# A third block size for the expert remainders of a routed expert layer: 192 rows with the weights held still in both layers

## The chip, the core and the metric

The kernel runs on one core of a Trainium2 chip. The metric is device time in microseconds (us) of one execution, taken as the median of several. The core has a matrix engine (TensorE, PE in the profile, with its weight loads listed apart as PEld), a vector engine (VectorE, DVE), a scalar engine (ScalarE, ACT), a general engine (GpSimd, POOL) and a synchronising engine (SyncE, SP) that issues most transfers. Results of PE land in eight banks called ps.

## The reference: windowed attention, then one expert per token

Attention over 8 batches and 8 heads comes first: 512 local queries, each with a window of 32 positions to both sides and 32 global keys, and 32 global queries that see all 544 keys. Its output is a matrix of 4352 rows (8 batches of 544 tokens) and 512 columns. Then every row goes through one of eight experts:

```python
for b in range(B):
    prev_e = -1
    for s in range(S):
        fresh_e = int(np.argmax(logits[b, s]))
        if s == 0 or local_gate[b, s] < 0.5:
            e = fresh_e
        else:
            e = prev_e if prev_e >= 0 else fresh_e
        prev_e = e
        ...
        h = np.maximum(x[b, s] @ w1[e], 0.0)
        out[b, s] = p[e] * (h @ w2[e])
```

Layer 1 (`w1`) takes 512 columns to 1024, layer 2 (`w2`) takes 1024 back to 512. How many rows an expert gets depends on the data. The reference's own inputs give the eight experts 710, 117, 1115, 689, 344, 287, 433 and 657 rows. Cut into blocks of 256 this makes 13 full blocks, and a remainder for each expert of 198, 117, 91, 177, 88, 31, 177 and 145 rows.

## The kernel before: attention, routing, then 21 blocks of rows

**Stages.** The first part (`Attn`) computes the attention and writes its rows, with each row's gate probabilities and number, to a table in memory (`xs`). `Route` then finds for every row its expert and its place, and makes lists of row numbers, one list for each block of at most 256 rows of one expert. `Moe` works through the blocks in a fixed order of slots: three full blocks that begin before the routing is finished, then the eight remainders with full blocks between them, then the other full blocks, as many as the routed counts call for. The remainder blocks stand at places 3, 5, 7, 9, 11, 13, 15 and 17 of the order, one for expert 0 to 7, each followed by a full block.

**One block.** `gather` (L1113) fetches the block's rows by indirect transfers into two tiles `xr`, 128 rows each. `xpose` (L1124 to L1131) turns each by four transposes on PE into columns, and stores them as a rounded part `xh` (ACT, L1126) and the rest `xl` (DVE, L1127). Both are in fp32r, a 32-bit format that PE takes at another pace than plain f32; the profile prints f32 for both. The weights come as eight pieces of 128x1024 from memory and are split in the same way, `hi` by ACT (L1089) and `lo` by DVE or POOL (L1098). A product of two split numbers is three matmuls: hi with hi, lo with hi, hi with lo.

**Layer 1, `mm1`** (L1159). For each of eight groups `fc` of 128 hidden columns, 12 matmuls hold a 128x128 piece of the weights and stream 256 columns, the block's rows. ACT takes the sum with a relu into `hh` (L1161), DVE keeps the rest in `hl` (L1162).

**Layer 2, `mm2`** (L1170). Here `hh` and `hl` are held, 128 rows of the block at a time, and 512 columns of the weights are streamed: 24 matmuls for the first 128 rows, 24 for the other 128. `store` (L1179, L1180) scales the result on ACT and scatters it to the output by an indirect transfer on POOL.

**What sets the order.** All is written out by hand. `whole` runs a block of up to 256 rows: layer 1, the first 24 matmuls of layer 2 with the next block's two `xpose` calls after groups 1 and 3 and its next-but-one `gather` (`ahead`) after group 3, the first `store`, the other 24 matmuls, the second `store`. `hook` runs after each group and makes the next weight piece ready, by the table `SP`. `half` runs a remainder of at most 128 rows in another way: it holds `xh` and `xl` in layer 1 and streams 256 columns of weights (L1233), turns the hidden values back on PE (L1222), and runs 24 matmuls of layer 2.

**The choice at run time.** `block` reads the remainder's row count into a register on every engine. With more than 128 rows, `whole` runs, and else `half`. Both are compiled, one behind the other, for each of the eight remainders.

**Banks.** The results of layer 1 rotate over three banks (`ph`), those of layer 2 over three others (`py`), and the transposes use two (`xtp`).

## Time and profile before

| | us |
|---|---|
| median of three runs | 728.29 |
| the three runs | 728.14, 728.29, 732.7 |
| the execution that was profiled: its own time | 726.73 |
| its span, first to last instruction | 725.0 |
| what lies around the span | 1.73 |

In the profile, PE is busy for 694.1 us of the span, DVE for 494.5, ACT for 410.8 and POOL for 249.5. The granted TensorE clock is 0.99 of full speed over the span. A row of the groups of instructions gives the line in the code, the engine, the operation, the tiles, the shapes, how many there are, the busy time and the mean duration of one. The duration of a matmul or a weight load on PE is longer than the distance to the next one, since they are pipelined: how fast PE goes is read from the starts, or from a run of many.

### The profile page before, as it was taken

How to read it: one execution, taken by the hardware profiler on the slowest of the kernel's cores; microseconds unless marked ns; L12 is line 12 of the kernel's file. 1: busy time of each engine (PE TensorE's matmuls, PEld its weight loads, DVE VectorE, ACT ScalarE, POOL GpSimd, SP SyncE). 2: the span in 40 equal slices, each digit the busy share in tenths (PEclk: the TensorE clock that was granted, in tenths of full speed). 3: DMA queues.
4: the chain of work that ended last, by engine and by line, in shares of the span. 5: the costliest groups of instructions: out<-in, count | busy, mean ns of one | idle time of the engine just before them, and what ended most of it. 6: DMA issues, size and time to landing. Idle time of an engine off the chain costs nothing.

```text
span 725.0 us, 19621 instructions
## 1 busy us (share of the span) xinstructions
PE 694.1 (96%) x7797; PEld 591.5 (82%) x7797; DVE 494.5 (68%) x1203; ACT 410.8 (57%) x724; POOL 249.5 (34%) x337
## 2 busy tenths in 40 slices
PE   9999999999899988899999999999999999999991
PEld 7777777777677767789989898898989988998891
DVE  7868778778888578885557675565858456645570
ACT  4555565554555636455467675566766455645560
POOL 6634434433243555523132332314232322312210
PEclk9999999999999999999999999999999999999996
DMA  8966886866594676675678787767878677567772
GB/s 314 377 248 230 318 288 249 324 251 239 191 350 157 212 240 211 227 252 177 224 246 301 266 295 246 214 216 260 288 270 283 227 239 239 189 212 238 237 207 109
DMA packets 50575, 178.74 MB, mean 247 GB/s; under 512 B 8733, under 2 KB 10013, under 8 KB 46368
## 3 DMA queue, kind: packets, MB, share of 16 engines
q1 hardware_dynamic: 43456, 155.76, 62.2%
q0 software_dynamic: 6720, 21.36, 8.4%
q8 instruction: 71, 1.16, 0.6%
q14 instruction: 40, 0.33, 0.2%
q10 hardware_dynamic: 288, 0.13, 0.1%
HBM read 158.84 MB, written 19.42 MB: 246 GB/s over the span
## 4 chain that ended last, share of the span: by engine, by line
PE 57%; DVE 5%; issue 1%; DMA 1%; POOL 1%; ACT 0%; POOLq 0%; ACTq 0%; SPq 0%
PE ps L1170 26%; PE ps L1159 25%; PE ps L1233 3%; PE ps L1124 2%; DVE wp L1098 2%; DMA raw<-in_w_dram 1%; DVE key L739 0%; PE ps L1222 0%; DVE hl L1162 0%; DVE cid L1011 0%; PE ps L987 0%; POOL out_dram L1180 0%; DVE cid L998 0%; DVE bs L919 0%; DVE nbc L916 0%
## 5 line engine op out<-in xcount | busy, mean ns | idle before, releaser
L1089 ACT CAST wp<-raw 128x1024 fp32r<-128x1024 f32 x176 | 182.9, 1049 | 33.8 <-DMA raw<-in_w_dram 32.6
L1170 PE MATMUL ps<-wp,hh 128*128 128x512 f32 x608 | 195.1, 402 | 0.0
L1098 DVE TENSOR_TENSOR wp<-raw,wp 128x1024 fp32r<-128x1024 f32 x154 | 188.2, 1230 | 8.4 <-ACT wp L1089 7.9
L1159 PE MATMUL ps<-xh,wp 128*128 128x256 f32 x1088 | 154.8, 284 | 6.5 <-DVE hl L1162 5.8
L1159 PEld LDWEIGHTS ps<-xh,wp 128*128 128x128 f32 x1088 | 141.1, 190 | 10.0 <-DVE hl L1162 7.1
L1162 DVE SCALAR_TENSOR_TENSOR hl<-ps,hh 128x256 fp32r<-128x256 f32 x136 | 56.9, 421 | 118.1 <-ACT hh L1161 118.1
L1113 POOL DMA_INDIRECT xr<-xs,idx x46 | 59.9, 1303 | 204.6 <-PE ps L1124 126.5
L1170 PEld LDWEIGHTS ps<-wp,hh 128*128 128x128 f32 x608 | 109.3, 188 | 21.6
L1170 PE MATMUL ps<-wp,hl 128*128 128x512 f32 x304 | 120.3, 396 | 0.0
L1161 ACT ACTIVATE hh<-ps 128x256 fp32r<-128x256 f32 x136 | 51.0, 383 | 75.6 <-PE ps L1159 71.3
L1159 PE MATMUL ps<-xl,wp 128*128 128x256 f32 x544 | 87.4, 283 | 0.0
L190 POOL TENSOR_SCALAR_AFFINE_SELECT qbd<-raw 64x512 f32<-64x512 f32 x62 | 44.5, 718 | 120.3 <-PE ps L242 98.4
L1159 PEld LDWEIGHTS ps<-xl,wp 128*128 128x128 f32 x544 | 74.7, 190 | 0.0
L1098 POOL TENSOR_TENSOR wp<-raw,wp 128x1024 fp32r<-128x1024 f32 x21 | 54.8, 2612 | 51.4 <-ACT wp L1089 19.5
L242 PE MATMUL ps<-kx,qbd 128*64 128x128 f32 x1024 | 71.5, 281 | 0.9 <-issue 0.9
L1180 POOL DMA_INDIRECT out_dram<-y,tk x38 | 40.7, 1072 | 81.7 <-ACT y L1179 66.4
L1170 PEld LDWEIGHTS ps<-wp,hl 128*128 128x128 f32 x304 | 57.1, 188 | 13.6
L242 PEld LDWEIGHTS ps<-kx,qbd 128*64 128x64 f32 x1024 | 55.3, 138 | 11.9 <-issue 7.8
L247 DVE TENSOR_REDUCE mx<-ps 128x4 f32<-128x512 f32 x64 | 43.9, 685 | 27.9 <-PE ps L242 27.8
L253 ACT ACTIVATE pe<-pe 128x512 f32<-128x512 f32 x64 | 40.7, 636 | 29.8 <-DVE pe L249 29.8
L1179 ACT ACTIVATE y<-ps,pp 128x512 f32<-128x512 f32 x38 | 26.0, 685 | 53.3 <-issue 46.9
L249 DVE TENSOR_TENSOR pe<-ps,mx 128x512 f32<-128x512 f32 x64 | 44.0, 688 | 1.6
(214 smaller groups left out, 841.4 us busy)
## 6 DMA issues: line engine op xcount, KB each, us to landing
raw<-in_w_dram SPq DMA_DIRECT2D x179, 512.0 KB, 4.4
v<-in_vw_dram SPq DMA_DIRECT2D x32, 1040.0 KB, 9.2
raw<-in_qk_dram SPq DMA_DIRECT2D x32, 528.0 KB, 7.1
xs<-xa SPq DMA_DIRECT2D x8, 1056.0 KB, 4.7
qgb<-in_qg_dram SPq DMA_DIRECT2D x8, 128.0 KB, 4.2
xr<-xs,idx POOLq DMA_INDIRECT x46, 6.3
out_dram<-y,tk POOLq DMA_INDIRECT x38, 5.6
xs<-xg SPq DMA_DIRECT2D x32, 16.0 KB, 4.1
```

What stands on the lines that cost most here:

```text
L190: self.nc.gpsimd.affine_select(out=out, in_=in_, pattern=pat, compare_op=ALU.is_ge, fill=0.0, base=0, channel_multiplier=0)
L242: nc.tensor.matmul(sp[64 * t2:64 * t2 + 64, t], qbd[:, w], kf[:, f:f + P], start=False, stop=True, skip_group_check=True)
L247: nc.vector.tensor_reduce(out=mx, in_=st["sp"], axis=AX.X, op=ALU.max)
L249: nc.vector.tensor_tensor(out=st["pe"][:, 4 * hb:4 * hb + 4], in0=st["sp"], in1=mx.broadcast_to([P, 4, P]), op=ALU.subtract)
L253: self.nc.scalar.activation(out=pe, in_=pe, func=AF.Exp, scale=SCALE)
L1089: nc.scalar.copy(out=hi, in_=raw)
L1098: (nc.gpsimd if pool else nc.vector).tensor_tensor(out=lo, in0=raw, in1=hi.bitcast(F32), op=ALU.subtract)
L1113: self.nc.gpsimd.indirect_dma_start(out=self.xr[j], out_offset=None, in_=src, in_offset=bass.IndirectOffsetOnAxis(ap=self.rt.idx[:, 2 * i ...
L1159: nc.tensor.matmul(ph, a[:, dc, fs], b_[:, dc], start=(n == 0), stop=(n == 11))
L1161: nc.scalar.activation(out=self.hh[:, fc], in_=ph, func=AF.Relu)
L1162: nc.vector.scalar_tensor_tensor(out=self.hl[:, fc], in0=ph, scalar=0.0, in1=self.hh[:, fc].bitcast(F32), op0=ALU.max, op1=ALU.subtract)
L1170: nc.tensor.matmul(py, a[:, fc, js], b_[:, fs], start=(fc == 0 and k == 0), stop=(fc == 7 and k == 2))
```

## The change: at most 192 rows in a block of its own

A constant `PART = 192` is added. Where a remainder has more than 128 rows, `block` now asks a second time: over 192 rows `whole` runs as before, and with 129 to 192 rows the new function `part` runs.

`mm1` gets a width `n`. In `part` it streams 192 columns in place of 256, and its ACT and DVE results are 192 columns wide. In layer 2 `part` holds the weights, 128x128 at a time, and streams 192 columns of `hh` and `hl`, so that the output comes out turned (columns of the output on the partitions, rows of the block along the free side). It goes in two passes `d` over two groups of 128 output columns each, and each pass fills one bank of `py`. ACT and DVE copy the two halves of a bank to the tile `yT`, which is the `xT` tile of the attention used again. Then `back` turns them by transposes with `idf` into the layout that `store` wants: those of pass 0 stand after group 4 of pass 1, those of pass 1 at the end. Two banks of the `ph` rotation take the turned result, and both `store` calls stand at the end of the block. The next block's first `xpose` stands after group 3 of pass 0, its second one behind pass 1, and `ahead` after it.

```diff
+PART = 192
...
-    def mm1(self, i, fc):
+    def mm1(self, i, fc, n=256):
...
-        ph = self.ph()[:, 0:256]
-        n = 0
+        ph = self.ph()[:, 0:n]
+        hh, hl = self.hh[:, fc, 0:n], self.hl[:, fc, 0:n]
+        g = 0
         for a, b_ in ((hi, self.xh), (lo, self.xh), (hi, self.xl)):
             for dc in range(4):
-                nc.tensor.matmul(ph, a[:, dc, fs], b_[:, dc], start=(n == 0), stop=(n == 11))
+                nc.tensor.matmul(ph, a[:, dc, fs], b_[:, dc, 0:n], start=(g == 0), stop=(g == 11))
...
+    def part(self, i, n):
+        nc = self.nc
+        yT = self.yT
+        for fc in range(8):
+            self.mm1(i, fc, n)
+            self.hook(i, fc)
+        out = []
+
+        def back(c):
+            for j in range(2):
+                nc.tensor.transpose(out[j][:, P * c:P * c + P], yT[:, c, P * j:P * j + P], self.cst.idf)
+        for d in range(2):
+            py = self.py().rearrange("p (c t) -> p c t", c=2)
+            for fc in range(8):
+                hi, lo = self.wp[8 * i + 4 + fc // 2]
+                for c in range(2):
+                    f0 = 512 * (fc % 2) + P * (2 * d + c)
+                    for k, (a, b_) in enumerate(((hi, self.hh), (lo, self.hh), (hi, self.hl))):
+                        nc.tensor.matmul(py[:, c, 0:n], a[:, f0:f0 + P], b_[:, fc, 0:n], start=(fc == 0 and k == 0 and c == 0), stop=(fc == 7 and k == 2),
+                                         skip_group_check=True)
+                if d == 0:
+                    self.hook(i, 8 + fc)
+                    if fc == 3:
+                        self.xpose(i + 1, 0)
+                elif fc == 4:
+                    out += [self.ph() for _ in range(2)]
+                    back(0)
+                    back(1)
+            nc.scalar.copy(out=yT[:, 2 * d, 0:n], in_=py[:, 0, 0:n])
+            nc.vector.tensor_copy(yT[:, 2 * d + 1, 0:n], py[:, 1, 0:n])
+        self.xpose(i + 1, 1)
+        self.ahead(i)
+        back(2)
+        back(3)
+        for j in range(2):
+            self.store(out[j], j)
...
                 self.rem = len(self.wp) + 1
-                self.whole(i)
+                with self.tc.If(self.cv[1 + SLOT[i] - NX] > PART) as full:
+                    self.whole(i)
+                end = self.state()
+                self.reset(st)
+                with full.Else():
+                    self.part(i, PART)
...
+    moe.yT = at.xT
```

**How the order of instructions moves, on PE.** In the names, ps with a number is a bank, wp a split weight piece, hh and hl the two parts of the hidden values, xr the fetched rows of the next block, idf the identity, and xT the tile that holds the turned output. A name stands before a comma where it is streamed, behind it where it is held. In the block of expert 3 before, layer 2 begins with these rows:

```order
L1159 MATMUL ps_66<-xl,wp_4208 128x256 x4
L1170 MATMUL ps_63<-wp_4209,hh 128x512 x2
L1170 MATMUL ps_63<-wp_4209,hl 128x512
L1170 MATMUL ps_63<-wp_4209,hh 128x512 x2
L1170 MATMUL ps_63<-wp_4209,hl 128x512
L1124 MATMUL ps_68<-idf,xr_86 128x128 x4
```

In the new function, the same place of the same block, for one weight piece:

```order
L1161 MATMUL ps_66<-xl,wp_4208 128x192 x4
L1277 MATMUL ps_63<-hh,wp_4209 128x192 x2
L1277 MATMUL ps_63<-hl,wp_4209 128x192
L1277 MATMUL ps_63<-hh,wp_4209 128x192 x2
L1277 MATMUL ps_63<-hl,wp_4209 128x192
L1277 MATMUL ps_63<-hh,wp_4209 128x192 x2
L1277 MATMUL ps_63<-hl,wp_4209 128x192
L1277 MATMUL ps_63<-hh,wp_4209 128x192 x2
L1277 MATMUL ps_63<-hl,wp_4209 128x192
```

Held and streamed operands have changed places, and where a weight piece had six matmuls of 512 columns in a pass, it has twelve of 192.

The second place is ACT at the end of the same block. Before, it ends so:

```order
L1126 CAST xh<-ps_67 128x4x128
L1089 CAST wp_101<-raw_78 128x1024
L1089 CAST wp_4207<-raw_79 128x1024
L1089 CAST wp_4208<-raw_80 128x1024
L1179 ACTIVATE y_4318<-ps_63,pp_92 128x512
L1179 ACTIVATE y_4319<-ps_64,pp_92 128x512
L1295 UNCONDITIONAL_BRANCH
```

and in the new function so:

```order
L1090 CAST wp_101<-raw_78 128x1024
L1090 CAST wp_4207<-raw_79 128x1024
L1090 CAST wp_4208<-raw_80 128x1024
L1287 COPY xT<-ps_63 128x192
L1287 COPY xT<-ps_64 128x192
L1127 CAST xh<-ps_67 128x4x128
L1181 ACTIVATE y_4318<-ps_69,pp_92 128x512
L1181 ACTIVATE y_4319<-ps_65,pp_92 128x512
L1336 UNCONDITIONAL_BRANCH
```

The cast that makes the second half of the next block's `xh` has moved from the middle to behind the weight casts and two new copies, and the first store from the middle to the end.

More of the change, by code (lines that the diff above doesn't have):

```diff
@@ L1154, in mm1 @@
         fs = slice(P * (fc % 2), P * (fc % 2) + P)
-        ph = self.ph()[:, 0:256]
-        n = 0
+        ph = self.ph()[:, 0:n]
+        hh, hl = self.hh[:, fc, 0:n], self.hl[:, fc, 0:n]
+        g = 0
         for a, b_ in ((hi, self.xh), (lo, self.xh), (hi, self.xl)):
             for dc in range(4):
-                nc.tensor.matmul(ph, a[:, dc, fs], b_[:, dc], start=(n == 0), stop=(n == 11))
-                n += 1
-        nc.scalar.activation(out=self.hh[:, fc], in_=ph, func=AF.Relu)
-        nc.vector.scalar_tensor_tensor(out=self.hl[:, fc], in0=ph, scalar=0.0, in1=self.hh[:, fc].bitcast(F32), op0=ALU.max, op1=ALU.subtract)
+                nc.tensor.matmul(ph, a[:, dc, fs], b_[:, dc, 0:n], start=(g == 0), stop=(g == 11))
+                g += 1
+        nc.scalar.activation(out=hh, in_=ph, func=AF.Relu)
+        nc.vector.scalar_tensor_tensor(out=hl, in0=ph, scalar=0.0, in1=hh.bitcast(F32), op0=ALU.max, op1=ALU.subtract)
     def mm2(self, i, py, fc, j):
@@ L1296, in block @@
                 self.rem = len(self.wp) + 1
-                self.whole(i)
+                with self.tc.If(self.cv[1 + SLOT[i] - NX] > PART) as full:
[4 more added lines that the diff above has]
+                    self.part(i, PART)
+                assert len(self.wp) == len(end[1]) and self.nld == end[2]
                 self.rem = -1
```

## The prediction

> **What bounds the kernel now.** I read the shares of the engines first, then the chain that ended last.
>
> ```profile
> PE 694.1 (96%) x7797; PEld 591.5 (82%) x7797; DVE 494.5 (68%) x1203; ACT 410.8 (57%) x724; POOL 249.5 (34%) x337
> ...
> PE ps L1170 26%; PE ps L1159 25%; PE ps L1233 3%; PE ps L1124 2%; DVE wp L1098 2%; DMA raw<-in_w_dram 1%; DVE key L739 0%; PE ps L1222 0%; DVE hl L1162 0%; DVE cid L1011 0%; PE ps L987 0%; POOL out_dram L1180 0%; DVE cid L998 0%; DVE bs L919 0%; DVE nbc L916 0%
> ```
>
> Half of the chain is the two layers on PE. How many blocks of each kind ran follows from the groups of layer 1.
>
> ```profile
> L1159 PE MATMUL ps<-xh,wp 128*128 128x256 f32 x1088 | 154.8, 284 | 6.5 <-DVE hl L1162 5.8 <-POOL wp L1098 0.6
> L1159 PE MATMUL ps<-xl,wp 128*128 128x256 f32 x544 | 87.4, 283 | 0.0
> L1233 PE MATMUL ps<-wp,xh 128*128 128x256 f32 x128 | 18.6, 287 | 0.0
> ```
>
> 1088 + 544 matmuls at 96 a block are 17 blocks in `whole`. `half` has 32 of its hi pieces a block on this row, so 128 are 4 blocks. That fits the row counts: four remainders are at most 128. Of the four above, 198 stays in `whole`, and 177, 177 and 145 (experts 3, 6 and 7) are to go through `part`. **Three blocks change.** Counted along the chain they are places 9, 15 and 17, each followed by a full block. The first of them, in the chain in order of time (start, us, what):
>
> ```profile
> 448.13 11.49 PE ps L1159 x96
> 459.63 1.41 PE ps L1170 x6
> 461.04 0.44 PE ps L1124 x4
> 461.47 1.40 PE ps L1170 x6
> 462.87 0.44 PE ps L1124 x4
> 463.31 8.39 PE ps L1170 x36
> ```
>
> All three, as stretches (PE busy is the first number behind the length):
>
> ```profile
> 448.13:471.69 23.56, 23.56 (x155) 21.29 (x154) 12.95 (x23) 13.16 (x20) 7.10 (x5) 1.00 0.67 205
> 568.84:592.40 23.56, 23.56 (x155) 21.28 (x154) 12.94 (x23) 13.15 (x20) 7.11 (x5) 1.00 0.65 214
> 615.81:639.31 23.50, 23.50 (x155) 21.22 (x154) 12.94 (x23) 13.16 (x20) 7.11 (x5) 1.00 0.68 217
> ```
>
> PE is busy for the whole of each stretch at full clock, while DVE and ACT need 13 us of 23.5. So only PE's time counts here: 23.54 us a block in the mean.
>
> **What a matmul of 192 columns costs.** The chain gives two widths: 11.49 / 96 = 0.1197 us from one to the next at 256 columns, 8.39 / 36 = 0.2331 at 512. A line through both has 0.000443 us a column, and 192 columns lie on it at 0.1197 - 64 x 0.000443 = 0.0913 us. That is the pace if streaming sets it. But each of these matmuls holds other weights than the one before it, in `part` in layer 2 too (hi, lo, hi). So the load of 128 weight columns has to fit into the same distance. Three rows show how long it takes:
>
> ```profile
> 391.80 0.30 PEld L1159 LDWEIGHTS ps<-xh,wp 128*128 128x128 f32 x2 [0.32 <-DVE hl L1162]
> ...
> 174.65 0.96 PEld L831 LDWEIGHTS ps<-idf,sc 5*128 5x128 f32 x8 [0.17 <-issue]
> ...
> 174.65 1.05 PE L831 MATMUL ps<-idf,sc 5*128 5x5 f32 x8
> ...
> L1159 PEld LDWEIGHTS ps<-xh,wp 128*128 128x128 f32 x1088 | 141.1, 190 | 10.0 <-DVE hl L1162 7.1 <-POOL wp L1098 1.0
> ...
> L831 PEld LDWEIGHTS ps<-idf,sc x16: 181/187/187, 174.6 to 266.4; 5*128 5x128 f32 x8, 3*128 3x128 f32 x8
> L831 PE MATMUL ps<-idf,sc x16: 247/248/269, 174.6 to 266.4; 5*128 5x5 f32 x8, 3*128 3x3 f32 x8
> ```
>
> The first is a restart after a wait, where nothing else was in flight: two fp32r loads take 0.30 us together and 0.19 each, so the second starts 0.11 us after the first. The L831 rows are plain f32, with 128 weight columns and only five streamed: streaming costs next to nothing, and still eight loads start (0.96 - 0.187) / 7 = 0.110 us apart, the matmuls (1.05 - 0.248) / 7 = 0.115 us. Loads do not run ahead side by side. At 256 columns the load hides under 0.1197 us; at 192 streaming would need 0.0913 and the load 0.110. **I take 0.111 us**, bounded below by 0.108 (the load alone, rounding down), and above by 0.1197, what the 256-column matmul takes with both at work.
>
> [...]
>
> **The sum for one block.** Layer 1 falls from 11.49 us to 96 x 0.111 = 10.66, a gain of 0.83. Layer 2 falls from 1.41 + 1.40 + 8.39 = 11.20 to 96 x 0.111 = 10.66: twice as many loads, a gain of 0.54. The next block's eight transposes stay, at 2 x 0.44. Eight `back` transposes of the same shape are new, 0.88 us. Then there is the handover. Its rows:
>
> ```profile
> L1124 PE MATMUL ps<-idf,xr 128*128 128x128 f32 x176 | 26.6, 273 | 0.0
> L1126 ACT CAST xh<-ps 128x512 fp32r<-128x512 f32 x44 | 25.9, 588 | 19.8 <-ACT wp L1089 11.7 <-PE ps L1124 7.8
> L1161 ACT ACTIVATE hh<-ps 128x256 fp32r<-128x256 f32 x136 | 51.0, 383 | 75.6 <-PE ps L1159 71.3 <-ACT wp L1089 1.1
> L360 ACT COPY xgT<-ps 128x128 f32<-128x128 f32 x8 | 2.1, 265 | 2.4 <-PE ps L358 2.4
> L303 DVE TENSOR_REDUCE m<-ps 128x1 f32<-128x256 f32 x16 | 6.7, 418 | 0.4 <-PE ps L295 0.3
> L1127 DVE TENSOR_TENSOR xl<-ps,xh 128x512 fp32r<-128x512 f32 x44 | 30.1, 685 | 3.0 <-ACT xh L1126 3.0
> L1179 ACT ACTIVATE y<-ps,pp 128x512 f32<-128x512 f32 x38 | 26.0, 685 | 53.3 <-issue 46.9 <-PE ps L1170 5.6 <-DVE xl L1127 0.9
> ```
>
> The next block's first matmul needs the whole `xh`, and its second half is now made last. From the start of those four transposes it takes 0.33 + 0.27 us until the last has landed, then 0.59 for the cast: 1.19. PE has 0.44 + 0.44 = 0.88 us of transposes in that time. So it idles 0.31, with the signal between engines about **0.36 us**; between 0 (if the pieces overlap better) and 0.7 (if copy and cast queue up). The new copies are 192 columns, between 265 and 383 ns on ACT and under 418 on DVE; those of pass 1 are covered by the four transposes ahead of `back(2)`, and their excess by the range. `xl` follows 0.69 us after the cast and is first needed eight matmuls on, 0.96 us, so it hides.
>
> Together 10.66 + 10.66 + 0.88 + 0.88 + 0.36 = 23.44 us against 23.54: **0.10 less a block, 0.3 in three**.
>
> **What I cost at nothing.** The copies of pass 0 stand behind the last weight casts. There was slack at that point, as the end of the first of the three blocks shows:
>
> ```profile
> 467.12 0.69 ACT L1179 ACTIVATE y<-ps,pp 128x512 f32<-128x512 f32 x1
> ...
> 471.78 0.69 ACT L1179 ACTIVATE y<-ps,pp 128x512 f32<-128x512 f32 x1 [3.97 <-issue]
> ...
> 473.57 0.42 DVE L1162 SCALAR_TENSOR_TENSOR hl<-ps,hh 128x256 fp32r<-128x256 f32 x1 [6.08 <-ACT hh L1161]
> ```
>
> The first 24 matmuls of layer 2 end at 463.31 + 12 x 0.233 = 466.1. ACT was through with the casts and the store by 467.81, 1.7 us later, and then idled 3.97; DVE idled 6.08. `back(0)` comes 30 matmuls, 3.3 us, into pass 1, so the copies are there. If that cover were gone, PE would stand as long as the casts are late. The two stores together keep ACT for 1.37 us at the end; behind them waits the next block's first relu, which is due after 12 matmuls, 1.44 us, and PE goes on through three banks before it needs it. On POOL the gathers move some 8 us later, ahead of both scatters: two issues and the landing are
>
> ```profile
> L1113 POOL DMA_INDIRECT xr<-xs,idx x46 | 59.9, 1303 | 204.6 <-PE ps L1124 126.5 <-PE ps L1170 31.4 <-issue 21.3
> ...
> xr<-xs,idx POOLq DMA_INDIRECT x46, 6.3
> ```
>
> 2 x 1.3 + 6.3 = 8.9 us, and the rows are first needed 11.49 + 1.41 = 12.9 us into the next block. The scatters behind them have nobody waiting but the y tiles, of which there are three. SP issues the same eight weight loads in the same order, and is only led past one more branch. The jump over `whole` costs nothing on PE: into `half`, the same kind of jump, PE went without a gap.
>
> ```profile
> 365.96 8.34 PE ps L1170 x36
> 374.30 2.86 PE ps L1233 x24
> ```
>
> **Forecast: no change that can be measured.** From the profiled execution, 726.73 us (1.73 of it outside the span, untouched) becomes 726.4. The median of the runs shown lies 1.56 above it; less 0.3 it gives **728.0 us**. A measurement of this kernel can tell about 1%, 7.3 us, from no change.
>
> **The rivals.**
>
> *Streaming sets the pace.* Loads would hide even at 192 columns: 192 x 0.0913 = 17.53 us for both layers, the block 17.53 + 1.76 + 0.36 = 19.65, so 3.9 less, 11.7 in three, and the time **716.6 us**. For it speaks that the 256- and 512-column rows lie so near a line through zero. Against it speak the three load rows: it would need a load under 0.092 us. [...]
>
> *Narrow fp32r goes at the pace of f32 (the slower side).* No fp32r row of this trace streams fewer than 256 columns. The plain f32 transposes take 0.44 / 4 = 0.110 us for 128 columns, 0.00086 a column, near twice the fp32r pace. If PE treats 192 columns of fp32r like that, a matmul takes 0.165 us, both layers 31.7, the block 33.8: 10.3 more, 30.8 in three, **759.1 us**. It decides as soon as a matmul passes 0.124 us, where a block is 2.4 us longer and three reach the 1%. Against it: f32 and fp32r loads of 128 columns take the same 187 and 190 ns, and nothing in the rows shows a step with the width.
>
> *A costly handover.* ACT runs in order, and in `part` the copy of pass 0, that of pass 1 and the cast of `xh` all stand behind the last weight casts, which wait for memory. If these are more than 3.3 us late into pass 1, PE stands at `back(0)` and again at the end, 2 to 3 us a block, 7.5 in three: **735.5 us**. Against it stand the 3.97 and 6.08 us of idle above.
>
> *It is not reached.* If the counts on the chip differed, `part` would not run, and the time stays 728.3. The four `half` blocks speak for the counts.
>
> **How the numbers follow.** Forecast 0.77, streaming 0.08, narrow fp32r 0.07, handover 0.06, not reached 0.02. The forecast's own range: with 0.108 us and no handover three blocks lose 0.3 + 1.7 + 1.1 = 3.1 us, with 0.1197 and 0.7 they gain 5.0 + 1.0 - 0.3 = 5.7, so 725 to 734. To leave out no more than the two far cases and half a point of noise, the range is 722 to 737 us: forecast, handover and not reached, 0.85. Faster by over 1% is streaming and a corner of the forecast, 0.09. Slower by over 1% is narrow fp32r and half of the handover with a corner, 0.12. The rest, 0.79, is within 1%.
>
> **What would show it.** In the new profile: L1277 with 288 matmuls and 288 more on layer 1's line at 192 columns; 96 of them in 10.4 to 11.5 us (0.108 to 0.1197 each), with weight loads that follow one another without a gap; eight transposes more a block; a wait of 0.2 to 0.7 us of the following block's first matmul on ACT's `xh`. Layer 1 of such a block in 8.8 us would mean streaming, in 15.8 narrow fp32r. I am wrong if the three blocks are over 1 us shorter or over 2 us longer than 23.5.

## The result, and the profile after

The changed kernel took 760.79 us (median of four: 754.81, 758.81, 762.78, 768.3), the kernel before 730.5 beside it. The ratio is 1.039, with an interval of 1.030 to 1.048: **slower by 28 to 30 us**, where 728.0 was forecast in a range of 722 to 737. Two slow executions of this study, the 768.3 here and a single 970.43 of a later kernel (the three sizes with `half` in the middle), are in no ratio. The profiled execution took 754.81 us with a span of 753.1.

First the page, PE's share and the shares of the chain that ended last by engine:

```profile
PE 701.1 (93%) x7965; PEld 600.4 (80%) x7965; DVE 494.2 (66%) x1209; ACT 413.0 (55%) x730; POOL 250.6 (33%) x337
...
PE 52%; DVE 6%; issue 5%; DMA 2%; ACT 2%; POOL 1%; SPq 0%; ACTq 0%; POOLq 0%
```

PE is busy for 7.0 us more than before (only 0.7 of them in the three rewritten blocks, as the next rows show), but the span is 28.1 longer: PE stands for 52 us of it, where it stood for 31. "issue" has 5% of the chain, time in which an engine waited for nothing that the profile shows.

Then the three blocks that the change is about, as stretches, each from its first matmul to the next block's:

```profile
463.27:486.89 23.62, 23.62 (x209) 23.00 (x207) 12.43 (x22) 12.79 (x21) 4.80 (x3) 1.00 0.71 234
595.61:619.37 23.76, 23.76 (x209) 23.00 (x208) 12.40 (x22) 12.79 (x22) 4.79 (x3) 1.00 0.73 238
642.76:667.02 24.26, 23.91 (x210) 23.05 (x208) 12.83 (x22) 13.11 (x22) 4.48 (x3) 1.00 0.70 233
```

They take 23.62, 23.76 and 24.26 us against 23.56, 23.56 and 23.50 before: 1.0 us more in all three. The first of them along the chain:

```profile
463.43 10.70 PE ps L1161 x96
474.13 2.68 PE ps L1277 x24
476.81 0.44 PE ps L1125 x4
477.25 6.01 PE ps L1277 x54
483.26 0.48 PE ps L1269 x4
483.74 1.99 PE ps L1277 x18
485.74 0.44 PE ps L1125 x4
486.17 0.80 PE ps L1269 x4
```

Layer 1 takes 10.70 / 96 = 0.1115 us a matmul, and layer 2 takes 2.68 + 6.01 + 1.99 = 10.68. The forecast had 10.66 for each. **So 27 of the 28 us lie outside the blocks that the change rewrites.** Where they lie is seen by laying the starts of the blocks side by side. The two kernels stand together at 327.18, the start of expert 0's block. The next block starts at 350.87 before and 354.35 after (3.5 us later), the first `half` at 374.14 and 382.23 (4.6 more), the full block behind the second `half` at 424.26 and 439.78 (7.4 more), and the last one at 686.12 and 713.93: 27.8 us. All of it is at `half` blocks, at expert 0's end, and in the blocks right behind them.

What stands there shows in the groups of matmuls, shapes apart. The last numbers of a row are PE's idle time just ahead and what ended it:

```profile
L1277 PE MATMUL ps<-hh,wp 128*128 128x192 f32 x192 | 33.0, 276 | 0.0
L1277 PE MATMUL ps<-hl,wp 128*128 128x192 f32 x96 | 26.3, 274 | 0.0
...
L1235 PE MATMUL ps<-wp,xh 128*128 128x256 f32 x128 | 21.2, 314 | 11.6 <-issue 11.6
```

`half`'s first layer, not a line of which was changed, has 11.6 us of idle ahead of it; the same group had 0.0 before. In the timeline of PE, the end of a full block and the start of the second `half`:

```profile
421.67 0.40 PE L1172 MATMUL ps<-wp,hl 128*128 128x512 f32 x1
425.15 1.19 PE L1235 MATMUL ps<-wp,xh 128*128 128x256 f32 x8 [3.08 <-issue]
```

No other engine is waited for. What PE's sequencer did in that time is in the rows of the two lines that choose the path. First L1295 of the kernel before, then L1334 (over 128 rows?) and L1336 (over 192 rows?) after; the numbers are the shortest, median and longest in ns:

```profile
L1295 PEldq COMPARE_BRANCH  x12: 70/293/439, 327.0 to 635.0; - x12
```

```profile
L1334 PEldq COMPARE_BRANCH  x8: 70/3270/6848, 326.8 to 639.0; - x8
```

```profile
L1336 PEldq COMPARE_BRANCH  x8: 65/327/7618, 327.0 to 666.2; - x8
```

A branch that isn't taken costs 65 to 92 ns. Taken ones of these lines cost up to 0.44 us before; after, the four jumps into `half` cost 6.4 to 6.8 us each and the jump out of expert 0's block 7.6. The rows of the two pairs of `half` blocks:

```profile
L1334 PEldq COMPARE_BRANCH  x2: 6447/6648/6848, 375.6 to 418.1; - x2
...
L1334 PEldq COMPARE_BRANCH  x2: 6527/6647/6767, 506.6 to 549.2; - x2
```

The second of these began at 418.1, when PE still had matmuls until 422.07; it ended at 424.98, and PE started at 425.15. So some 3.9 us of such a jump lie under PE's own backlog and 3 stand as idle time. **Five long jumps for 27 us: 5 to 6 us each**, twice what PE idles at the jump. The rest follows right behind. Here are the stretches behind the five jumps (first the block behind expert 0's, then the starts of the four `half` blocks), and below them the first two `half` blocks of the kernel before; the last three columns are the granted clock, the share of busy transfers, and GB/s:

```profile
354.35:358.35 4.00, 4.00 (x21) 4.00 (x22) 1.19 (x2) 0.39 (x1) 0.00 (x0) 0.59 0.10 37
382.23:386.84 4.61, 4.61 (x27) 4.61 (x27) 0.00 (x0) 1.32 (x2) 0.00 (x0) 0.63 0.25 98
425.15:428.26 3.11, 3.11 (x27) 3.11 (x27) 0.00 (x0) 1.32 (x2) 0.00 (x0) 1.00 0.29 113
513.49:517.85 4.36, 3.35 (x27) 3.15 (x27) 0.00 (x0) 1.32 (x2) 0.00 (x0) 1.00 0.21 83
555.92:560.53 4.61, 4.61 (x27) 4.61 (x27) 0.00 (x0) 1.32 (x2) 0.00 (x0) 0.63 0.26 100
```

```profile
374.14:377.00 2.86, 2.86 (x25) 2.86 (x24) 0.00 (x0) 1.87 (x3) 0.99 (x1) 1.00 1.01 401
411.19:414.10 2.91, 2.91 (x26) 2.90 (x25) 0.00 (x0) 1.90 (x3) 1.00 (x1) 1.00 0.97 366
```

The first 24 matmuls took 4.61 us in place of 2.86 at 382 and at 556, with a granted clock of 0.63, and 3.11 at 425. The one at 513 holds a second wait of 1.0 us. The clock fell behind three of the five jumps, though PE had stood for about as long at each (3.3, 2.7 and 2.8 us at these, 3.1 and 3.0 at the other two). Laid out block by block, the 26.8 us outside the three blocks are 14.8 us more of idle PE at the five jumps, 5.9 more inside the four `half` blocks, and 6.1 us by which PE is busy longer with the same matmuls, nearly all of it in these stretches. And the transfers, at full share at this point before, are down to a quarter: a weight piece is fetched into a buffer that an earlier piece has to leave first, and with PE standing none do. That is argued from the order of the loads; what the profile shows is that the time is missing at the end of the block (1.0 to 1.4 us of the idle PE in each `half`), where the chain of after goes over the weights:

```profile
434.01 4.65 DMA raw<-in_w_dram
438.68 1.05 ACT wp L1090
439.78 11.59 PE ps L1161 x96
```

Four of the `half` blocks end on such a wait now; before, one did.

**Theory A**: `part` itself is as forecast, but its code lies inside each remainder's choice, so the jumps that lead past it have become too long for what PE's sequencer has fetched ahead. That it fetches ahead, and how far, is a supposition at this point. That PE can take this long over a jump was in the profile of before: the last branch of the block loop, which leads past the slots that stay empty, took 7051 ns, with no matmul of PE behind it to lose the time.

```profile
L1317 PEldq COMPARE_BRANCH  x5: 65/65/7051, 635.8 to 712.7; - x5
```

The rivals of theory A are **B**, that `part`'s own work (its copies, later casts and stores) holds up what comes behind, and **A2**, that every further branch, or the longer program as such, costs.

### The profile page after: what moved, and what is told of

The parts are those of the page before. It is cut to its first block, busy times and chain, and to the rows that moved or that the text cites. A ratio compares the mean times of both kernels' runs of the same rounds, so it can differ in the third digit from the quotient of the medians.

```text
span 753.1 us, 19989 instructions
## 1 busy us (share of the span) xinstructions
PE 701.1 (93%) x7965; PEld 600.4 (80%) x7965; DVE 494.2 (66%) x1209; ACT 413.0 (55%) x730; POOL 250.6 (33%) x337
## 3 DMA queue, kind: packets, MB, share of 16 engines
q8 instruction: 80, 1.31, 0.7%
## 4 chain that ended last, share of the span: by engine, by line
PE 52%; DVE 6%; issue 5%; DMA 2%; ACT 2%; POOL 1%; SPq 0%; ACTq 0%; POOLq 0%
PE ps L1161 25%; PE ps L1172 16%; PE ps L1277 4%; PE ps L1235 3%; DMA raw<-in_w_dram 2%; DVE wp L1099 2%; PE ps L1125 2%; ACT wp L1090 1%; PE ps L1269 1%; ACT y L1181 0%; ACT hh L1226 0%; DVE key L740 0%; DVE cid L1012 0%; DVE hl L1164 0%; PE ps L988 0%
## 5 line engine op out<-in xcount | busy, mean ns | idle before, releaser
L1161 PE MATMUL ps<-xh,wp 128*128 128x256 f32 (+1 forms) x1088 | 154.5, 284 | 15.0 <-DVE hl L1164 5.7
L1172 PE MATMUL ps<-wp,hh 128*128 128x512 f32 x512 | 164.5, 402 | 0.0
L1164 DVE SCALAR_TENSOR_TENSOR hl<-ps,hh 128x256 fp32r<-128x256 f32 (+1 forms) x136 | 55.6, 409 | 112.5 <-ACT hh L1163 112.5
L1172 PEld LDWEIGHTS ps<-wp,hh 128*128 128x128 f32 x512 | 92.0, 188 | 18.0
L1172 PE MATMUL ps<-wp,hl 128*128 128x512 f32 x256 | 101.2, 395 | 0.0
L1163 ACT ACTIVATE hh<-ps 128x256 fp32r<-128x256 f32 (+1 forms) x136 | 51.0, 376 | 89.4 <-PE ps L1161 85.4
L1161 PE MATMUL ps<-xl,wp 128*128 128x256 f32 (+1 forms) x544 | 87.0, 282 | 0.0
L243 PE MATMUL ps<-kx,qbd 128*64 128x128 f32 x1024 | 71.1, 281 | 1.1 <-issue 1.1
L1172 PEld LDWEIGHTS ps<-wp,hl 128*128 128x128 f32 x256 | 48.1, 188 | 11.5
```

The costliest lines, as they stand in the source:

```text
L243: nc.tensor.matmul(sp[64 * t2:64 * t2 + 64, t], qbd[:, w], kf[:, f:f + P], start=False, stop=True, skip_group_check=True)
L1161: nc.tensor.matmul(ph, a[:, dc, fs], b_[:, dc, 0:n], start=(g == 0), stop=(g == 11))
L1163: nc.scalar.activation(out=hh, in_=ph, func=AF.Relu)
L1164: nc.vector.scalar_tensor_tensor(out=hl, in0=ph, scalar=0.0, in1=hh.bitcast(F32), op0=ALU.max, op1=ALU.subtract)
L1172: nc.tensor.matmul(py, a[:, fc, js], b_[:, fs], start=(fc == 0 and k == 0), stop=(fc == 7 and k == 2))
```

## The experiments

In what follows the program is measured in matmuls that a jump leads past, later in PE's instructions, as the compiled program has them: each matmul is two (the page counts 7965 on PE and 7965 on PEld), the branches come on top. `whole` is 152 matmuls, `half` 88, `part` 208. With the branches and labels counted in, two instructions to a matmul, the text and the expectations call them 152 to 154, 92 and 209.

**`part` is compiled but never runs.**

```diff
-PART = 192
+PART = 128
```

> The limit of the new function is set to 128 rows, so it is compiled but never runs, and all remainders over 128 rows go through whole as before. Theory A (jumps): PE runs dry where a taken branch leads over a whole and a part together, or over a part and a half; in the changed kernel such a jump into half cost about 5.8 us with its restart, and the one at the end of whole 3.5 us. Here there are four of each: 728.3 + 4 x 5.8 + 4 x 3.5 = about 766 us, more than the changed kernel. Theory B (the new function's own work: its late xh, its gathers and stores moved to the end, the weights behind it): 728 to 730 us, since it never runs. Theory C (a second branch costs by itself, wherever it leads): the four blocks that meet it are some 0.1 us longer each, 729 us.

Measured: 782.38 us (two runs), ratio 1.071 (1.061 to 1.081). The three remainders of 145 to 177 rows run through `whole` again, as before, and the loss has nearly doubled.

```profile
L1334 PEldq COMPARE_BRANCH  x8: 70/3247/7380, 327.6 to 656.7; - x8
L1336 PEldq COMPARE_BRANCH  x8: 65/3652/7701, 327.7 to 679.8; - x8
```

Four long jumps into `half` (6.4 to 7.4 us), and now four long ones out of `whole` past `part` and `half` (7.2 to 7.7) in place of one: eight for 51.6 us of span, 6.45 each. B falls: code that isn't run costs more than code that is. Theory A had said 766: it had counted these eight jumps, but at 5.8 and 3.5 us each.

**The routing is fixed in the program.** Each remainder calls its path directly, in the kernel before and in the changed one. Both hold for the row counts of these inputs alone.

```diff
-            with self.tc.If(self.cv[1 + SLOT[i] - NX] > P) as big:
+            n = [198, 117, 91, 177, 88, 31, 177, 145][SLOT[i] - NX]
+            if n <= P:
+                self.half(i)
+            else:
...
-                with self.tc.If(self.cv[1 + SLOT[i] - NX] > PART) as full:
-                    self.whole(i)
...
+                self.part(i, PART) if n <= PART else self.whole(i)
```

> The kernel before with the choice between whole and half fixed from this data's row counts (198, 117, 91, 177, 88, 31, 177, 145), so that no remainder has a branch. It gives the right output for this routing only. Theory A: the short jumps of the kernel before cost nothing, 727 to 729 us. Rival A2: each branch has a price even there, some us less than before.

> The changed kernel with its choice fixed in the same way: whole for expert 0, part for experts 3, 6 and 7, half for the others, no branch at a remainder. It gives the right output for this routing only. Theory A: all of the loss goes, and what is left is part's own price, 0.1 to 0.3 us a block: 728 to 730 us, within 0.2% of the run with the fixed routing of before. Theory B (part's own work): 755 us.

Measured: 730.01 us for the kernel before (ratio 0.998, 0.995 to 1.001), 732.98 for the changed one (1.001, 0.998 to 1.004), ten runs each. Both are 1 to 3 us over theory A's ranges; the kernel before took 731.89 beside them. All of the loss is gone, and the short jumps cost nothing that can be measured. The `half` group and the three blocks of the changed kernel with the routing fixed:

```profile
L1235 PE MATMUL ps<-wp,xh 128*128 128x256 f32 x128 | 18.6, 287 | 0.0
```

```profile
453.24:476.76 23.52, 23.52 (x209) 23.02 (x207) 12.49 (x22) 12.78 (x21) 4.82 (x3) 1.00 0.66 222
573.71:597.35 23.64, 23.64 (x209) 23.00 (x207) 12.40 (x22) 12.67 (x21) 4.80 (x3) 1.00 0.64 224
620.73:644.68 23.95, 23.65 (x210) 23.02 (x208) 12.92 (x22) 13.15 (x22) 4.79 (x3) 1.00 0.65 220
```

Without jumps they take 71.1 us against 70.6 in `whole`: 0.5 more in three, where 0.3 less was forecast. From the start of expert 0's block to that of the last block the two profiles need 359.3 us (before) and 359.5 (changed). The two profiled executions are 4.5 us apart: 2.8 of that stand ahead of this stretch and 1.5 behind its end, where the programs are the same. That start lies between 326 and 334 in the profiles of this study.

**Shorter jumps by another layout.** Two kernels set the pieces out in other ways: one asks for over 192 rows first, so that each jump leads past one piece only; the other gives each size an If of its own.

```diff
-            with self.tc.If(self.cv[1 + SLOT[i] - NX] > P) as big:
...
+            with self.tc.If(c > PART) as full:
                 self.rem = len(self.wp) + 1
-                with self.tc.If(self.cv[1 + SLOT[i] - NX] > PART) as full:
-                    self.whole(i)
+                self.whole(i)
...
+            with full.Else():
+                with self.tc.If(c > P) as big:
...
+                    self.part(i, PART)
...
+                with big.Else():
+                    self.half(i)
```

> The same three functions, asked in another order: over 192 rows first (whole), then over 128 (part), else half. The way into half leads over whole and then over part, in two jumps, each over one function. Only the end of whole (expert 0) still leads over two, part and half. Theory A: 728.3 + 1.0 for the three part blocks + 3.5 = about 733 us if a jump over part alone (208 matmuls) is still short; about 756 if it is not. Theory B: 755 to 760 us, as the same functions run on the same rows. Theory C: as B or more, since half now also meets two branches.

> The three functions stand one behind the other, each in an If of its own (part in two), so that every taken jump leads over one of them. Theory A: 728.3 + 1.0 = 729 to 730 us, no measurable difference from the kernel before; if a jump over part alone is long, four or five such jumps, 750 to 757 us. Theory B: 755 to 760 us. Theory C: more than 760 us, since every block meets four branches.

Measured: 777.47 us (1.067, 1.060 to 1.074) and 782.51 (1.068, 1.061 to 1.075). Both expectations of A missed: it got worse. In the second, PE also waits 0.9 to 1.3 us at the joins of the extra Ifs in the blocks of experts 3, 6 and 7, where no jump is long. In the first kernel the jump past `part` was long 4 times of 4 (3.5 to 8.3 us), the one past `whole` ahead of it short in five of seven (0.32 to 0.36) and long in two (7.1 and 7.5), and where both were long PE stood for 7.0 and 7.5 us. `half` has 24 us of idle ahead of it:

```profile
L1235 PE MATMUL ps<-wp,xh 128*128 128x256 f32 x128 | 24.3, 346 | 24.0 <-issue 24.0
```

So 154 matmuls are short in one place and long in another, in one and the same program. "How long is too long" had no single answer, and that was open from here on.

**The kernel before, with matmuls that never run.** Behind `whole`, in the same branch, 48 (and in a later kernel 24) matmuls under a condition that never holds; the jump into `half` leads past 203 (and 178).

```diff
                 self.whole(i)
+                end = self.state()
+                with self.tc.If(self.cv[1 + SLOT[i] - NX] > 254):
+                    for fc in range(4):
+                        self.mm1(i, fc)
                 self.rem = -1
```

> The kernel before, with 48 matmuls of layer 1 (and what ACT and DVE do with them) behind whole in an If that is never true, and no part. The jump into half now leads over 152 + 48 = 200 matmuls instead of 152. Theory A: if 200 are within reach, 728 to 733 us and PE's branch into half takes 0.3 to 0.4 us; if not, four long jumps, about 751 us, with 6 to 7 us in that branch. Theories B and C: 728 to 730 us, since nothing new runs.

> The kernel before with 24 matmuls behind whole that never run (a condition on over 254 rows): the jump into half leads past about 178 matmuls instead of 154. At 154 all four were short in the kernel before, at 203 two of four were long. Theory A: none to two of the four over 1 us, each of them with some 3 us of idle PE and 6 us of time; the time 730 to 748. If any dead piece with its extra branch costs as such, it would be as in e4_before_with_48_dead_matmuls, 760.

Measured, one run each: 762.25 and 748.15 us, beside 729.09 and 731.55 of the kernel before. With no third size at all the loss is there. At 203 the jumps took 7178, 1374, 1953 and 7545 ns, at 178 they took 313, 6178, 343 and 318, with PE idle for 2.42 us at the second and again at the fourth, though that branch was short. Each run of `whole` also waits 0.5 to 1.3 us at its end, at the extra If, so these kernels show the mechanism and not its price.

**Cut between the layers.** The choice is made twice, once for each layer, so that no jump leads past more than 153 matmuls, and none on the way through a `half` past more than 113; in a second kernel the 192 columns are used in layer 1 alone, and layer 2 is that of `whole`.

```diff
+            with self.tc.If(c > PART) as full:
...
+                self.first(i, 256)
...
+            with full.Else():
+                with self.tc.If(c > P) as big:
...
+                    self.first(i, PART)
...
+                with big.Else():
+                    rest = self.half(i)
...
+            with self.tc.If(c > PART) as full:
+                self.whole(i, False)
...
+            with full.Else():
+                with self.tc.If(c > P) as big:
+                    self.part(i, PART)
...
+                with big.Else():
+                    rest()
```

> The change with each of its three functions cut between the layers: first the layer 1 of whole, part or half is chosen, then the layer 2 of the same one, over 192 rows asked first each time. The work is the same. No jump of PE leads over more than some 150 matmuls (96 and 96 into the first piece of half, 56 and 112 into its second). Theory A, in the form that the jump's length counts (up to about 154 matmuls always or mostly short, from about 200 mostly long): 729 to 735 us, every branch on PE under 0.5 us, no idle of 3 us ahead of half. Rival A2, that any jump costs once there are many branches, or that the program's whole length counts: as long as the change or longer, 755 to 780 us.

> Only layer 1 has the third size (192 columns); layer 2 is that of whole or of half, and the two layers are chosen apart as in the kernel before this one. The longest way is 150 matmuls. Theory A: the three blocks lose 11.49 - 10.70 = 0.79 us each, 2.4 in all, and have none of the eight transposes and no late xh: 726 to 727 us, 2 us under the kernel before if all jumps are short. Rival A2: 755 us or more.

Measured: 763.52 us (1.043, 1.036 to 1.051) and 748.46 (1.025, 1.018 to 1.031). Theory A missed both times; the first lies in A2's range, the second 7 us under it. The way into `half` is two jumps of 97 right behind one another:

```profile
L1339 PEldq COMPARE_BRANCH  x9: 92/330/3938, 331.7 to 650.2; - x9
L1346 PEldq COMPARE_BRANCH  x10: 70/296/7673, 379.4 to 662.7; - x10
```

On this way the first, L1339, took 0.22 to 0.34 us each time, and the second, 0.4 us later, 6565, 7673, 418 and 3347 ns. So two short steps without work between them can cost what one long one costs, and did in three of four cases. Layer 1 alone at 192 columns is worth something: its three blocks take 22.80 us each, 0.7 less than before, which the jumps eat up.

**The same, with `half` in the middle.** The pieces of the last two kernels in another order (whole, half, part), so that `half` is led past less at a time, and has work between the jump in and the jump out.

```diff
             with full.Else():
-                with self.tc.If(c > P) as big:
+                with self.tc.If(c < P + 1) as small:
+                    rest = self.half(i)
...
+                with small.Else():
...
                     self.first(i, PART)
...
-                with big.Else():
-                    rest = self.half(i)
```

> Same instructions, same three sizes and the same two choices per block (one at each layer) as in e5_cut_at_the_layer; only the order in which the pieces stand in the program differs: whole, half, part in both layers, so that half lies in the middle and no path is led past more than 154 matmuls at a time, two jumps in a row counted together (e5: up to 195). Theory A (what costs is how far a taken jump leads beyond what PE's sequencer has already fetched): no jump into or out of half over 1 us, no weight wait behind it, the three part blocks 23.5 to 24.3 us, the time 730 to 738 us. Theory A2 (the number of branches, or the length of the program as a whole, costs): as e5, 760 to 767 us.

> The 192 columns in layer 1 alone, as in e6_layer_1_alone_cut, with the pieces in the order whole, half, part for layer 1 and half, whole for layer 2: half is led past 97 matmuls at most at a time, part past 145. The columns 192 to 255 of layer 2's rows come from an earlier block and fall on rows that are not stored. Theory A: no long jump but perhaps the one at expert 0's end; the three narrow blocks 22.8 us as in e6, 0.7 under the block before, so 726 to 733 us, within 1% of the kernel before. Theory A2: as e6, 745 to 752 us.

Measured: 749.95 us (1.023, 1.018 to 1.027) in place of 763.52, and 737.68 (1.008, 1.005 to 1.011) in place of 748.46. The layout alone, with the same instructions and the same number of branches, gives back 13.6 and 10.8 us, so A2 falls as the cause of the loss. But both came out above A's range. In the first, all jumps into `half` were short, and yet PE stood 2.45 and 2.23 us in two of the four at the cut, ahead of layer 2, right behind the two jumps there (one pair took 3.1 us, the other 0.3), and in three of the four it stood another 1.3 to 1.6 us later on:

```profile
432.73 0.30 PEld L1172 LDWEIGHTS ps<-wp,hh 128*128 128x128 f32 x2 [2.44 <-issue]
```

In the second, `half` has no idle left, but expert 0's jump out of its layer 1 still took 3.3 us, and each full block behind a `half` takes 24.4 to 24.7 us, up to a microsecond more than before, with ACT late at the first relu behind a weight cast that waits for memory. Its best block, 22.80 us, doesn't pay for that: no version of this study beats the kernel before by an amount that can be measured.

**One place of dead code, ahead of all remainders.** Every jump was now laid out by its place in the compiled program, counted in PE's instructions. Nearly all lone jumps fit one rule: with the program cut into pages of 256 instructions, a jump is long when its target is neither in the page that it starts from nor in the next one. By the rule the jump of 306 past `whole` is short if it starts in the first 206 instructions of a page, and long behind that. The rule rests on a fit of where the pages begin, so it was put to a test. In three kernels, 48, 84 or 120 dead matmuls in one place ahead of expert 0's block shift all that follows, and change nothing else but for the one If, at which PE stands once for 1.3 us in the first two.

```diff
             self.bound(1 + SLOT[i] - NX)
+            if SLOT[i] == NX:
+                with self.tc.If(self.cv[1] > 254):
+                    for fc in range(4):
+                        self.mm1(i, fc % 8)
+                self.reset(st)
```

> The kernel before with 48 matmuls that never run (a condition on over 254 rows) ahead of the first remainder block; behind them everything is the same, 98 PE instructions later, with the same jump into half over 306 instructions. Page theory (two pages of 256 instructions held, position counted from the fit over the twelve runs): the jumps of experts 1 and 2 start at positions 139 and 164 of their page and stay short (0.3 to 0.5 us), those of experts 4 and 5 start at 214 and 239, leave both pages and take 6 to 8 us, with 2.4 to 3.5 us of idle PE each ahead of half: 740 to 748 us. Length alone, or amount of code: all four short as before, or any other pattern; 728 to 735 us.

> The same with 84 dead matmuls, a shift of 170 instructions. Page theory: now experts 1 and 2 go long (positions 211 and 236, 6 to 8 us each), experts 4 and 5 (30 and 55) are short: 740 to 748 us. Length alone: all four short, 728 to 735 us; amount of dead code: worse than with 48.

> The same with 120 dead matmuls, a shift of 242 instructions, nearly a whole page. Page theory: positions 27, 52, 102 and 127, all four jumps into half short as in the kernel before; what is left is the one more condition and its jump over 242 instructions once: 729 to 736 us. Amount of dead code: the worst of the three, over 745 us.

The jumps into `half`, experts 1 and 2 in the first row of each pair and 4 and 5 in the second; shift 98, then 170, then 242:

```profile
L1300 PEldq COMPARE_BRANCH  x2: 313/320/328, 372.3 to 409.3; - x2
...
L1300 PEldq COMPARE_BRANCH  x2: 6610/6951/7292, 493.7 to 535.6; - x2
```

```profile
L1300 PEldq COMPARE_BRANCH  x2: 6617/6704/6790, 377.3 to 417.9; - x2
...
L1300 PEldq COMPARE_BRANCH  x2: 323/384/446, 506.1 to 543.2; - x2
```

```profile
L1300 PEldq COMPARE_BRANCH  x2: 318/369/420, 377.5 to 415.3; - x2
...
L1300 PEldq COMPARE_BRANCH  x2: 318/333/348, 499.5 to 536.5; - x2
```

Measured: 740.25 us (1.012, 1.006 to 1.018), 742.41 (1.015, 1.007 to 1.022) and 738.24 (1.010, 1.006 to 1.013). All twelve jumps went as the rule said, one by one, with the same length throughout: eight in 0.31 to 0.45 us, four in 6.6 to 7.3. Length alone and amount of code fall. The two long jumps cost 8.6 to 10.8 us in the stretch from the first full block behind expert 0 to the last block (335.25 us before, 346.04 and 343.88 with them). The third time is over its range of 729 to 736: its one jump past the dead piece, 242 instructions from the 15th of a page, took 2.6 us with 2.9 of idle, and expert 0's block 1.5 us more.

**Three widths, routing fixed.** What sets the pace of a narrow matmul was still argued rather than shown. `part` runs with 128, 224 and 240 columns for experts 3, 6 and 7; rows 129 and on of expert 3 are left out.

```diff
-                self.part(i, PART) if n <= PART else self.whole(i)
+                self.part(i, {3: 128, 6: 224, 7: 240}[SLOT[i] - NX]) if n <= PART else self.whole(i)
```

> The choice of the path is fixed in the program for this routing, and part runs with 128 columns for expert 3, 224 for expert 6 and 240 for expert 7; rows 129 and on of expert 3 are left out. The weight load sets the pace (forecast of this study): from one matmul to the next 0.108 to 0.112 us at 128 columns, 0.110 to 0.114 at 224, 0.111 to 0.117 at 240. Streaming sets the pace (rival): 0.063, 0.1055 and 0.1126 us on the line through the rows of 256 and 512 columns, so the block of expert 3 would have each layer in 6.0 us instead of 10.7. Narrow fp32r at the pace of f32: 0.110 at 128, but 0.19 at 224 and 0.21 at 240.

Layer 1 of the three blocks along the chain, 128, 224 and 240 columns:

```profile
451.25 10.67 PE ps L1161 x96
...
571.41 10.71 PE ps L1161 x96
...
618.47 10.75 PE ps L1161 x96
```

0.1111, 0.1116 and 0.1120 us a matmul. Nearly twice the columns cost 0.8% more time: streaming, which would have needed 6 us at 128 columns, does not set the pace up to 240 columns. Nor does a fixed price of every matmul with a load of its own: in the kernel before, 34 matmuls in bf16 with 128x128 weights each and 80 columns take 0.036 us apiece.

```profile
325.99 1.23 PE ps L987 x34
```

That leaves the load of 128 four-byte weight columns, as the rows of the prediction had it (0.110 us). No run here varies the width of the load itself.

## Why the prediction was wrong

**The step that failed** is in the part on what was costed at nothing: "The jump over `whole` costs nothing on PE: into `half`, the same kind of jump, PE went without a gap." The row behind it was right for the jump of 306 instructions that the kernel before has. The change has that jump too, into `part`, and there it stayed short three times of three (0.34 us). What the step overlooked is which jumps the change makes longer. The way into `half` led past `whole`; with `part` inside the same branch it leads past 725 instructions. The way out of `whole`, 183 instructions past `half`, becomes 600 past `part` and `half`. By the rule neither can be short anywhere, and none was: 13 of these in the changed kernel and in the one in which `part` never runs took 6.4 to 7.7 us each. The prediction counted the branch that was added, and not the ones whose target moved; of the eight remainders it looked at the three whose work changes, and the other five lost the time: five jumps of 6.4 to 7.6 us, 26.8 us in all, for a term that stood at nothing. The row of L1317 in the same profile, a jump past 1211 instructions that took 7.05 us, stood against it.

Taken over all profiles of the study, with one beginning of the pages for all programs, fitted on the first fourteen: 162 taken jumps lead past at least 98 instructions and don't follow another such jump within 8 us. Of these, 27 stay in their page and take 0.18 to 0.42 us, 86 end in the next one and take 0.18 to 0.45, and 45 go farther and take 3.3 to 8.2, mostly about 7. Four don't fit: one lies three instructions short of the limit and was long, and three begin within 15 instructions of the page's start, and took 1.4 to 2.6 us. The short branch of the run with 24 dead matmuls that had PE standing behind it landed 12 instructions ahead of the next page. The length of a page is in the jumps as well: 41 of them are those of the kernel before, of the changed one and of the one in which `part` never runs, and the twelve into `half` of the shifted kernels; of all lengths from 150 to 419, with the beginning left free, only 255 to 258 put each of the 41 on its side (240 misplaces three, 272 two).

The profile lists the transfers of instructions, before first, then after:

```profile
q8 instruction: 71, 1.16, 0.6%
```

```profile
q8 instruction: 80, 1.31, 0.7%
```

1.31 MB in 80 packets are 16.4 KB each (16,384 bytes in the trace). In the compiled program each instruction has 64 bytes (PE's 18,926 of the kernel before fill 1,211,264), so a packet is 256 of them, the page of the rule. The packets have their times in the trace, and these show the fetch itself. Inside the jump of 418.13 to 424.98, one falls into the window from 422.6 to 423.7:

```profile
q8 instruction: 1, 0.02, 5.5%
```

Each of the five long jumps of the changed kernel holds one such packet. It starts 4.0 to 5.3 us after the jump began, takes 0.95 to 0.98 us, and ends 1.3 to 1.5 us before the jump does. So does the jump past 1211 instructions in the kernel before: 0.88 us, 1.5 before the end. Of the 16 short taken jumps of the two kernels (0.19 to 0.44 us) none waits for one: 14 have none beside them, and two end 0.5 and 0.6 us ahead of the end of a packet already under way. So targets in the two pages were there already, and those beyond them were fetched. The jumps that don't fit for being near a page's start wait for a packet too: in the kernel with 48 dead matmuls one ends at 418.72, and the jump of 1374 ns at 420.08. So does PE behind the short branch of the run with 24: a packet runs from 546.01 to 546.98, and PE goes on at 548.44.

The size of the packets, the packet inside each long jump and the shifted kernels agree with the rule. The price of a long jump here is mostly 6 to 8 us in the sequencer, 2.4 to 3.8 us of idle PE, and 4.3 to 6.5 us of time.

**What was right.** *The pace.* 0.111 us was forecast for 192 columns because the load sets it; 0.1115 was measured in layer 1 and 10.68 / 96 = 0.1113 in layer 2, and the run with three widths rules streaming out. Both rivals on the pace fall with it. *The block.* 23.44 us was forecast; it took 23.5 to 24.0 with the routing fixed, and 23.6 to 24.3 with the jumps. *The handover* was of the right size, 0.36 us, and at another place: PE doesn't wait for `xh` at the next block's start, but ahead of the last four `back` transposes, 0.80 us in place of 0.44, for the copies of pass 1. *The cover* of pass 0's copies held in the main (0.48, 0.61 and 0.69 us in place of 0.44). The third block's further 0.3 us stand at the dynamic branch behind it.

**A number that looks right.** The measured 760.8 lies by the 759.1 of the rival by which narrow fp32r goes at the pace of f32. Its mark, layer 1 of such a block in 15.8 us, isn't there: it took 10.7. The time agrees by accident, and without the marks in "What would show it" the wrong cause would have been read out of it. Those marks came out as forecast, but for the wait on `xh`, and its sign of being wrong (blocks over 1 us shorter or 2 us longer) did not come, while the time was wrong, since they looked only at the blocks that the change rewrites.

**What stays open.** Why the clock fell behind three of the five long jumps and not behind the other two is not shown, nor is the way from the standing PE to the late weights, which was argued from the order of the loads. Of the 6 to 8 us of a long jump, the packet is 1 us, and some 1.4 us follow it; why it starts only 4 to 5 us after the jump began, and after 0.7 to 1.2 us in the jumps of 3.1 to 3.9 us, is not shown.

## What to carry to other kernels

When a change adds code to one side of a run-time choice, list every path that now has to be led past that code, above all those that run none of it, and measure the jumps in instructions: here PE's jumps past 306 instructions were short or long by where they stood, and all 13 past 600 and 725 were long, at 5.4 us of time each in the changed kernel (27 us for five) and 6.45 in the one in which `part` never runs. Two short jumps in a row need not help; with 8.6 us of work between them, as in the two kernels with `half` in the middle, all eight jumps out of `half`'s layer 1 were short. And the kernel before, with its jumps past 306 instructions, lost 8.6 to 10.8 us, over a per cent, when 98 or 170 instructions ahead of all of them made two of the jumps long, so a small loss from an unrelated edit is checked at the branches first.

## What the runs showed of the hardware

- A lone taken jump on PE past at least 98 instructions took 0.18 to 0.45 us if its target was in its own page of 256 instructions or the next, and 3.3 to 8.2 us if not (158 of 162); one that isn't taken took 65 to 92 ns. Each of the five long ones of the changed kernel holds a transfer of 16 KB of instructions, which takes 0.95 to 0.98 us and ends 1.3 to 1.5 us before the jump does. On the other four engines the same branches of the kernels before and after took 34 to 69 ns, taken or not.
- PE's sequencer was 3.9 us ahead of the matmuls at a jump of the changed kernel (it began at 418.13, the last matmul ahead of it ended at 422.07). Jumps under that length were free in these cases: those of 1374 and 1953 ns in the kernel with 48 dead matmuls left PE no idle time, and the kernel before gained nothing that can be measured from a fixed routing (0.998, 0.995 to 1.001).
- The granted clock was 0.59 to 0.63 over the 4.0 to 4.6 us behind three of the five long jumps, after 2.7 to 3.3 us of idle PE, and 1.00 behind the other two, after 3.0 and 3.1.
- fp32r matmuls with a new 128x128 weight each started 0.111 to 0.112 us apart at 128, 192, 224 and 240 columns, and 0.1197 at 256; bf16 ones with 128x128 weights and 80 columns started 0.036 apart.
